# Clearing padding rows on VectorE and ScalarE and reordering the prologue of a fused FFT mixing and SwiGLU kernel

## The chip, the cores and the metric

The kernel runs on one core of one Trainium2 chip. The metric is the device time of one execution in microseconds; a change is judged by the median of several runs. The profile is that of one more execution.

## The reference

```python
def _attn_ref(x):                       # x: 8 x 3008 x 256, float32
    X = np.fft.fft(x, axis=1)
    X = np.fft.fft(X, axis=2)
    return X.real

def _moe_ref(x, w_gate, w_val, w_out):  # x: 24064 x 256; d_ff = 1536
    g = x @ w_gate
    silu = g * (1.0 / (1.0 + np.exp(-g)))
    val = x @ w_val
    return silu * val @ w_out
```

The real part of a two-dimensional Fourier transform of each of the 8 batches is fed, row by row, to a gated feed-forward block. The transform along the 256 columns is linear and can be folded into the two input weight matrices; so the kernel multiplies those once by cosine and sine tables (giving the tiles Wp, Wq and the mirrored Wm) and has only the transform along the 3008 rows left to do per batch.

## The kernel before, in words

**Layout.** The 3008 rows of a batch are folded by symmetry into 188 rows, of which 128 go through the tile XA and 60 through XC. XC holds two batches, 64 partitions each, and 4 partitions of each 64 are padding that has to be zero. Batch 0 has its own small version of XC, called XC0: partitions 0 to 59 and 64 to 123 hold data, 60 and 124 hold the first rows of the sequence, and the remaining padding partitions hold zeros.

**Prologue (about the first 30 us).** All of it is written out by hand, in the order in which each engine executes it.

- SyncE (SP) and ScalarE issue the input transfers. SP: XA upper rows (L247), two of the four XA lower sets (L249), two clears of XC0 padding (L251, copied 64 floats at a time from one row of zeros in the tile `sel`), XC0's pieces (L260), XC0's two first rows (L261), two clears of XC padding (L264), then the loads of batch 1 (L140, L142, L144). ScalarE issues the other two XA sets (L249) and two XC0 pieces (L260). Transfers share eight completion semaphores in rotation, so a queue's later transfer also waits until the earlier one on its semaphore has landed.
- GpSimd makes index rows, the phases `turns` (L332), the products for the small tables (L390 to L394), the placing matrix putC (L395), and issues the first weights (`load_w(0)`, L360); then it folds (`fold_d`, L480) and issues the further weights.
- VectorE makes the phase steps (L301 to L318), the matrix putA (L320), the angles (L336, L340), and later the sums of placed and loaded rows (`sums`, L422: SA for XA, SC for XC0).
- ScalarE makes the sine and cosine tables Tab (L343, L346), their negated part (`opposite`, L352) and weighted part (`weigh_ce`, L355), the small tables CD and SDt (`d_tables`, L402 to L405), the bf16 copies of the folds (EOb, L481) and of XC0's sums (SBc, `halves`, L426 and L427).
- TensorE does warming matmuls (L288, L439), `place` (L413: XA by putA, XC0 by putC), then the first transform, whose even and odd halves (`eo` 0 and 1) each consist of `half_folded` (L468, from EOb) and `unfolded` (L475, from SBc), with `row0` (L581) for one extra row, and `half_w` (L447), which turns the first 512 columns of the two weight matrices into Wp and Wq in two halves. `transform` then copies (L612) and combines (L617) the accumulators into the tiles Pt (even) and Qt (odd).

**Main part.** A planner with costs and due times orders, for 50 tiles of up to 512 columns and 12 blocks of d_ff each, the gate and value products (L904), the activation and products on ScalarE, VectorE and GpSimd, the output products (L1144), the remaining weight transforms (L1335), the folds of later batches and their transforms (L1287). Its first matmul takes Pt and Wp (L904); it follows `half_w(1, 1)` on TensorE. The change doesn't touch it.

The order on TensorE around the change is this, before:

```python
    psC = place(XC0, putC, 2, ((psO, "o"),))
    half_folded(0, 2)
    ...
    for k, (pool, nm) in enumerate(((psV, "v"), (psG, "g"))):
        half_w(0, k, pool, nm)
    ...
    unfolded(0, SBc)
    transform(0, 0, (0,), acc)
    for q in range(2):
        row0(0, q, acc[1][q])
    unfolded(1, SBc)
```

Of the kernel before, what the change touches and what calls it, by code (L numbers as in the profile page):

```python
# [12 lines left out]
F32 = mybir.dt.float32  # L13
I32 = mybir.dt.int32
BF16 = mybir.dt.bfloat16
AF = mybir.ActivationFunctionType
Alu = mybir.AluOpType
# [14 lines left out]
def kernel(  # L32
# [8 lines left out]
    nc = tc.nc  # L41
    B, M, D = x.shape
    Dff = moe_w_gate.shape[1]
    P = 128
# [21 lines left out]
    NCR = GH - P  # L66
# [14 lines left out]
    psG = ctx.enter_context(tc.tile_pool(name="psG", bufs=3, space=bass.MemoryType.PSUM))  # L81
    psV = ctx.enter_context(tc.tile_pool(name="psV", bufs=3, space=bass.MemoryType.PSUM))
    psO = ctx.enter_context(tc.tile_pool(name="psO", bufs=2, space=bass.MemoryType.PSUM))
# [8 lines left out]
    zero = const.tile([P, 1], F32, name="zero")  # L92
    w0 = const.tile([P, 2, nF], F32, name="w0")
    sel = const.tile([P, P], BF16, name="sel")
    CD = const.tile([P, 2, P], BF16, name="CD")
    SDt = const.tile([P, 2, P], BF16, name="SDt")
# [5 lines left out]
    XC = const.tile([P, 8, 2, D], F32, name="XC")  # L102
# [14 lines left out]
    def rows_at(b, row, ap):  # L117
        return bass.AP(tensor=x.tensor, offset=(b * M + row) * D, ap=ap)

    def up_block(b, j, n):  # L120
        return rows_at(b, 2 * j - 1, [[2 * D, n], [R * D, 4], [1, 2 * D]])
# [91 lines left out]
    vts = nc.vector.tensor_scalar  # L213
    vtt = nc.vector.tensor_tensor
    vstt = nc.vector.scalar_tensor_tensor
    pts = nc.gpsimd.tensor_scalar
    ptt = nc.gpsimd.tensor_tensor
# [7 lines left out]
    XC0 = tp.tile([P, 4, 2, D], F32, name="XC0")  # L225
    W0 = [tp.tile([P, 2, T], BF16, name=f"W0{i}") for i in range(2)]
    putA = tp.tile([P, P], F32, name="putA")
    putC = tp.tile([P, P], F32, name="putC")
    df = tp.tile([P, P], F32, name="df")
    prod = tp.tile([P, 2, P], F32, name="prodd")  # L230
    rrd = tp.tile([P, 2, P], F32, name="rrd")
# [3 lines left out]
    q = nc.sync  # L235

    nc.vector.memset(zero, 0.0)
    nc.vector.memset(sel, 0.0)
    nc.scalar.activation(w0[:, 0, 0:1], zero, AF.Silu)
    zrow = sel.bitcast(F32)[1:2, :]  # L240

    def zeros(X, hi):
        dst = X.rearrange("p a q d -> p (a q d)")[64 * hi + NCR:64 * hi + 64, :]
        return dict(out=dst.rearrange("p (k n) -> p k n", n=P // 2),
                    in_=zrow.unsqueeze(1).to_broadcast([1, (64 - NCR) * dst.shape[1] * 2 // P, P // 2]))

    q.dma_start(out=XA3[:, 0:4, :], in_=up_block(0, 1, P))  # L247
    for a, eng in ((3, nc.scalar), (2, q), (1, nc.scalar), (0, q)):
        eng.dma_start(out=XA3[:, 4 + a, :], in_=down_set(0, a, JA, LA, NA))  # L249
    for hi in range(2):  # L250
        q.dma_start(**zeros(XC0, hi))  # L251

    def xc0(hi, what):
        if what == 2:
# [4 lines left out]
    for hi, what in ((0, 2), (1, 2), (0, 0), (1, 0), (0, 1), (1, 1)):  # L259
        (q, nc.scalar)[hi if what != 1 else 0].dma_start(**xc0(hi, what))  # L260
    q.dma_start(out=XC0[NCR:64 + NCR + 1:64, 0:2, 1],  # L261
                in_=rows_at(0, 0, [[2 * R * D, 2], [R * D, 2], [1, D]]))
    for hi in range(2):
        q.dma_start(**zeros(XC, hi))  # L264

    iota = dict(channel_multiplier=0, allow_small_or_imprecise_dtypes=True)
    pcol = tp.tile([P, 1], F32, name="pcol")
    pcol2 = tp.tile([P, 1], F32, name="pcol2")
# [23 lines left out]
    def col(name, n=1, dt=F32):  # L292
        small[name] = tp.tile([P, n], dt, name=name)
        return small[name]
# [12 lines left out]

    m_cols(0, pcol, LA, JA)
    vts(mM[:, 0:2], mm_[:, 0:2], scalar1=1.0 / M, scalar2=None, op0=Alu.mult)
    half = col("half")  # L310
    vts(half, pcol, scalar1=64.0, scalar2=-64.0, op0=Alu.is_ge, op1=Alu.mult)
    pc = col("pc")
# [4 lines left out]
    vtt(mm_[:, 3:4], mm_[:, 3:4], inside, op=Alu.mult)  # L317
    vts(mM[:, 2:4], mm_[:, 2:4], scalar1=1.0 / M, scalar2=None, op0=Alu.mult)  # L318
    nc.vector.memset(halfpi, math.pi / 2.0)
    vts(putA, putA, scalar1=pcol, scalar2=None, op0=Alu.is_equal)  # L320
    nc.vector.memset(EOf[:, 1, :, P:P + 1], 0.0)
    vts(m2, pcol, scalar1=0.0, scalar2=-2.0, op0=Alu.not_equal, op1=Alu.mult)
    vts(sgn, half, scalar1=1.0 / 32, scalar2=1.0, op0=Alu.mult, op1=Alu.add)
# [27 lines left out]
    def opposite(ch):  # L351
        nc.scalar.activation(Tab[:, ch, :, :, NCE:NOO - 1], Tab[:, ch, :, :, GH + 1:NCE], AF.Copy, scale=-1.0)  # L352

    def weigh_ce():
        nc.scalar.activation(Tab[:, 1, 1, :, 0:NCE], Tab[:, 1, 1, :, 0:NCE], AF.Copy, scale=wC)  # L355

    def load_w(fc):
        for i, src in ((0, moe_w_gate), (1, moe_w_val)):
            dst = W0[i] if fc == 0 else Wraw[i][:, :, (fc - 1) * T:fc * T]
            nc.gpsimd.dma_start(out=dst, in_=src.rearrange("(no p) f -> p no f", p=P)[:, :, fc * T:(fc + 1) * T])  # L360
# [15 lines left out]
    def ce_angles(ch):  # L376
        rr, ra = ce_angle[ch]
        angles(rr, kf, ch, ti[ch])
        magnitude(ra, rr)

    def ce_tables(ch):
        rr, ra = ce_angle[ch]
        sine(ch, 0, NCE, rr)
        cosine(ch, 0, NCE, ra)

    ce_angles(0)
    nc.vector.memset(Tab[:, :, :, :, NOO - 1:NOO], 0.0)
    ce_tables(0)
    for i, c_ in enumerate((pcol, pcol2)):
        pts(prod[:, i, :], df, scalar1=c_, scalar2=1.0, op0=Alu.mult, op1=Alu.mult)  # L390
    pts(rad.bitcast(I32), prod, scalar1=1.0 / D, scalar2=1.0, op0=Alu.mult, op1=Alu.mult)
    pts(rrd, rad.bitcast(I32), scalar1=-float(D), scalar2=1.0, op0=Alu.mult, op1=Alu.mult)
    load_w(0)
    ptt(rrd, rrd, prod, op=Alu.add)  # L394
    pts(putC, putC, scalar1=pcol, scalar2=1.0, op0=Alu.is_equal, op1=Alu.mult)  # L395
    ce_angles(1)
    ce_tables(1)
    nc.vector.memset(sel[0:1, :], 1.0)
    scd = 2.0 * math.pi / D * (1.0 - 2e-7)

    def d_tables():
        nc.scalar.activation(rad, rrd, AF.Abs)  # L402
        nc.scalar.activation(CD, rad, AF.Sin, scale=-scd, bias=halfpi)
        nc.scalar.activation(SDt, rrd, AF.Sin, scale=-scd, bias=zero)
        nc.scalar.activation(CD[:, :, 0:1], CD[:, :, 0:1], AF.Copy, scale=0.5)  # L405
# [12 lines left out]
    def sums(S, k, X, pss):  # L418
        n = len(pss)
        for a in range(n):  # L420
            down = X[:, 7 - a] if n == 4 else X[:, 2 + a]
            vtt(S[:, k, a], pss[a], down[:, ::-1, :], op=(Alu.add, Alu.subtract)[k])  # L422

    def halves(SB, S, k, a=0):

        nc.scalar.copy(SB[:, k, 0, a:a + 2], S[:, k, a:a + 2, :, P:0:-1])  # L426
        nc.scalar.activation(SB[:, k, 1, a:a + 2], S[:, k, a:a + 2, :, P:D], AF.Copy, scale=(-1.0 if k else 1.0))  # L427
# [13 lines left out]
    def half_w(h, k, pool, nm):  # L441
        ps = pool.tile([P, 2, T // 2], F32, name=nm)
        dst, tab = ((Wp, CD), (Wq, SDt))[k]
        fs = slice(h * T // 2, (h + 1) * T // 2)
        for gv in range(2):
            for no in range(2):
                nc.tensor.matmul(ps[:, gv, :], tab[:, no, :], W0[gv][:, no, fs], start=(no == 0), stop=(no == 1))  # L447
        if k:
            nc.scalar.copy(dst[:, :, fs], ps)
            pts(Wm[:, :, fs], dst[:, :, fs], scalar1=m2, scalar2=1.0, op0=Alu.mult, op1=Alu.mult)  # L450
        else:
            nc.vector.tensor_copy(dst[:, :, fs], ps)
# [17 lines left out]
    def unfolded(eo, SB):  # L470
        for q in range(2):
            for a in range(2):
                dst, rhs = set_cols(acc[eo][q], Tab[:, 1, q, eo], a)
                for hf in range(2):
                    nc.tensor.matmul(dst, SB[:, eo, hf, a, q, :], rhs, start=False, stop=(a == 1 and hf == 1),  # L475
                                     skip_group_check=True)

    def fold_d(eo, a0):
        s_ = SA[:, eo, a0:a0 + 2]
        ptt(EOA[:, eo, a0:a0 + 2, :, 0:P], s_[:, :, :, P:0:-1], s_[:, :, :, P:D], op=(Alu.add, Alu.subtract)[eo])  # L480
        nc.scalar.copy(EOb[:, eo, a0:a0 + 2], EOA[:, eo, a0:a0 + 2, :, 0:P])  # L481
# [29 lines left out]
    warm(20)  # L511
    sums(SA, 0, XA, psA)
    opposite(0)
    d_tables()
    for a in (0, 2):
        fold_d(0, a)
    sums(SA, 1, XA, psA)
    start_acc(0)
    half_folded(0, 0)
    psC = place(XC0, putC, 2, ((psO, "o"),))  # L520
    half_folded(0, 2)
    weigh_ce()
    opposite(1)
    for a in (0, 2):
        fold_d(1, a)
    load_w(1)
# [2 lines left out]
    start_acc(1)  # L529
    for a in (0, 2):  # L530
        half_folded(1, a)
    nc.vector.memset(SDt[:, :, 0:1], 1.0)
    hd = tp.tile([P, 2, 2, 1], F32, name="hd")
    ptt(hd, SA[:, 0, 0:2, :, 0:1], SA[:, 0, 2:4, :, 0:1], op=Alu.add)
    heads(nc.gpsimd, hd[:, 0], hd[:, 1], CEa)
    nc.gpsimd.tensor_copy(EOA[:, 0, :, :, P:P + 1], SA[:, 0, :, :, 0:1])
    heads(nc.gpsimd, SC[:, 0, 0, :, 0:1], SC[:, 0, 1, :, 0:1], CEc)
    sums(SC, 1, XC0, psC)
    halves(SBc, SC, 1)
    for k, (pool, nm) in enumerate(((psV, "v"), (psG, "g"))):  # L540
        half_w(0, k, pool, nm)
    load_w(2)
    nc.gpsimd.iota(kfO, pattern=[[4, G]], base=1, **iota)
    for ch in range(2):
# [28 lines left out]
    def row0(b, q, ps):  # L573
        CE = coef_a(b)[0]
        todo = [(CE[:, q, 0, k, P:P + 1], Tab[:, 0, q, 0, e], e) for k, e in ((0, E0), (1, E1))]
        if b:
            todo.append((stack_of(b, 0)[:, q, 0, P:P + 1], Tab[:, 1, q, 0, 0:NCE], slice(0, NCE)))
        else:
            todo += [(CEc[:, q, 0, k, 0:1], Tab[:, 1, q, 0, e], e) for k, e in ((0, E0), (1, E1))]
        for l, r_, cols in todo:  # L580
            nc.tensor.matmul(ps[0:1, cols], l, r_, start=False, stop=True, skip_group_check=True)  # L581
# [56 lines left out]
    transform(0, 0, (0,), acc)  # L638
    for q in range(2):
        row0(0, q, acc[1][q])  # L640
    unfolded(1, SBc)
    transform(0, 0, (1,), acc)
    half_w(1, 0, psO, "o")
# [879 lines left out]
```

## Time and profile before

| | |
|---|---|
| Median of 8 runs | 624.19 us (622.86 to 628.66) |
| Profiled execution | 623.59 us |
| Its span, first to last instruction | 621.8 us |
| TensorE busy | 603.8 us (97% of the span) |
| VectorE, ScalarE, GpSimd busy | 577.4, 527.3, 471.3 us |
| Mean granted TensorE clock | 0.994 |

The span is what the trace covers; the execution's own time is 1.8 us longer. A busy share over the whole span says little about the prologue: there TensorE waits for data, and in the rest it is nearly always busy.

### The profile page before, as it was taken

What the parts mean: (1) busy time and instruction counts of PE and PEld (TensorE: products, weight loads), DVE (VectorE), ACT (ScalarE), POOL (GpSimd) and SP (SyncE); (2) the same over time, 40 slices, a digit from 0 to 9 for tenths busy, and PEclk for the clock granted to TensorE, in tenths of its full rate; (3) what the DMA queues carried; (4) which work ended last, traced back from release to release, by engine and by line L of the source; (5) the groups of instructions that cost most, each with busy time, mean ns of one, the idle gap of its engine ahead of it and who ended that gap; (6) DMA issues with size and microseconds to landing.
All of it is one profiled execution on the core that took longest, in us unless ns stands there. A gap on an engine that the chain in (4) does not pass through costs nothing.

```text
span 621.8 us, 12518 instructions
## 1 busy us (share of the span) xinstructions
PE 603.8 (97%) x4012; PEld 395.4 (64%) x4073; DVE 577.4 (93%) x1054; ACT 527.3 (85%) x1001; POOL 471.3 (76%) x432
## 2 busy tenths in 40 slices
PE   7899989999999999999999999999999999999997
PEld 4445656666666666666666666666666666666676
DVE  7499969999999999999999999999999999999982
ACT  5487556789889899898898899998998988999994
POOL 8599688899797888987888778877787444446652
PEclk9799999999999999999999999999999999999999
DMA  9762545544523613454144122125121111211112
GB/s 222 103 109 57 157 113 153 151 137 118 146 61 89 142 45 105 131 136 130 50 102 137 52 58 76 57 68 164 45 60 52 45 50 46 61 41 56 59 52 78
DMA packets 51340, 57.74 MB, mean 93 GB/s; under 512 B 8002, under 2 KB 38346, under 8 KB 51274
## 3 DMA queue, kind: packets, MB, share of 16 engines
q1 hardware_dynamic: 47592, 53.69, 32.0%
q0 software_dynamic: 3184, 2.36, 3.0%
q10 hardware_dynamic: 498, 0.89, 0.5%
q8 instruction: 32, 0.52, 0.4%
q14 instruction: 34, 0.28, 0.2%
HBM read 29.39 MB, written 24.65 MB: 87 GB/s over the span
## 4 chain that ended last, share of the span: by engine, by line
PE 84%; DVE 6%; DMA 3%; issue 2%; SPq 2%; POOL 2%; ACT 2%; DVEq 0%; ACTq 0%; POOLq 0%
PE o L1144 35%; PE g L904 22%; PE v L904 19%; DVE es L1027 2%; PE g L1287 2%; PE o L1287 2%; DMA XC<-in_x_dram 1%; DMA XA<-in_x_dram 1%; DVE sv L1088 1%; SPq L142 1%; PE v L1144 1%; PE o L413 1%; SPq L140 1%; PE g L581 1%; DVE hp L942 0%
## 5 line engine op out<-in xcount | busy, mean ns | idle before, releaser
L1095 POOL TENSOR_TENSOR hm<-sv 128x1024 bf16<-128x1024 f32 (+2 forms) x133 | 247.3, 1860 | 120.0 <-ACT sv L1074 67.6
L1088 DVE SCALAR_TENSOR_TENSOR sv<-es,v 128x512 f32<-128x512 f32 (+2 forms) x266 | 178.0, 670 | 1.7 <-issue 0.6
L1098 DVE TENSOR_TENSOR hp<-sp,v 128x512 bf16<-128x512 f32 (+2 forms) x260 | 174.2, 670 | 3.2 <-ACT sp L1071 2.4
L1144 PE MATMUL o<-Wo,hm 128*128 128x256 bf16 (+1 forms) x1128 | 166.4, 273 | 0.7
L1144 PE MATMUL o<-Wo,hp 128*128 128x256 bf16 (+1 forms) x1104 | 165.6, 273 | 0.4
L1144 PEld LDWEIGHTS <-hp 128*128 128x128 bf16 (+2 forms) x1140 | 112.1, 99 | 62.5 <-issue 4.2
L1144 PEld LDWEIGHTS <-hm 128*128 128x128 bf16 (+2 forms) x1140 | 112.0, 98 | 61.3 <-issue 0.4
L1002 ACT ACTIVATE sp<-g 128x512 f32<-128x512 f32 (+2 forms) x202 | 119.8, 594 | 32.9 <-PE g L904 21.6
L1074 ACT ACTIVATE sv<-g 128x512 f32<-128x512 f32 (+2 forms) x202 | 131.5, 652 | 7.7 <-PE g L904 5.1
L904 PE MATMUL v<-Pt,Wp 128*128 128x512 bf16 (+2 forms) x283 | 106.0, 375 | 2.4 <-DVE hp L1098 0.9
L1027 DVE SCALAR_TENSOR_TENSOR es<-bc,w,v 128x512 f32<-128x512 bf16 (+2 forms) x140 | 102.0, 731 | 5.2 <-DMA bc<-br 3.6
L904 PE MATMUL g<-Pt,Wp 128*128 128x512 bf16 (+2 forms) x284 | 106.4, 375 | 0.3
L904 PE MATMUL g<-Qt,Wq 128*128 128x512 bf16 (+2 forms) x242 | 90.5, 374 | 0.3
L976 ACT ACTIVATE v<-bc,w 128x512 f32<-128x512 bf16 (+2 forms) x126 | 87.2, 692 | 0.4 <-DVE hp L1098 0.3
L904 PE MATMUL g<-Qt,Wm 128*128 128x512 bf16 (+2 forms) x219 | 82.0, 374 | 0.2
L1025 ACT COPY es<-v 128x512 f32<-128x512 f32 (+2 forms) x126 | 73.5, 583 | 3.2 <-PE v L904 2.7
L904 PEld LDWEIGHTS <-Wp 128*128 128x128 bf16 x576 | 56.2, 98 | 30.6 <-issue 4.8
L904 PE MATMUL v<-Qt,Wq 128*128 128x512 bf16 (+2 forms) x162 | 60.7, 375 | 2.3 <-DVE es L1027 2.1
L904 PEld LDWEIGHTS <-Wq 128*128 128x128 bf16 x450 | 44.0, 98 | 21.5 <-issue 1.3
L1150 ACT COPY ev<-o 128x512 f32<-128x512 f32 x89 | 53.3, 599 | 4.1 <-PE o L1144 2.7
L904 PE MATMUL v<-Qt,Wm 128*128 128x512 bf16 (+2 forms) x148 | 55.4, 374 | 0.5 <-DVE hp L942 0.5
L904 PEld LDWEIGHTS <-Wm 128*128 128x128 bf16 x372 | 36.4, 98 | 17.8 <-issue 0.2
(191 smaller groups left out, 706.4 us busy)
## 6 DMA issues: line engine op xcount, KB each, us to landing
out_dram<-ev SPq DMA_DIRECT2D x96, 128.0 KB
XA<-in_x_dram SPq DMA_DIRECT2D x30, 256.0 KB
XA<-in_x_dram SPq DMA_DIRECT2D x112, 64.0 KB
XC<-in_x_dram SPq DMA_DIRECT2D x31, 120.0 KB
XC<-in_x_dram SPq DMA_DIRECT2D x105, 32.0 KB
bc<-br SPq DMA_DIRECT2D x21, 128.0 KB
St<-Fc SPq DMA_DIRECT2D x14, 128.5 KB
out_dram<-ev SPq DMA_DIRECT2D x12, 120.0 KB
```

Source lines behind the costliest of these rows:

```text
L904: nc.tensor.matmul(ps[:, :n], Wt[:, gv, fs], src[:, :n], start=start, stop=stop, skip_group_check=True)
L976: nc.scalar.activation(T_[kv][:, :w], bc[t][:, :w], AF.Copy, scale=w0[:, 1, f:f + 1])
L1002: nc.scalar.activation(T_[ksp][:, :w], T_[kg][:, :w], AF.Silu)
L1025: nc.scalar.copy(T_[kes][:, :w], T_[kv][:, :w])
L1027: nc.vector.scalar_tensor_tensor(T_[kes][:, :w], bc[t][:, :w], w0[:, 1, f:f + 1], T_[kv][:, :w], op0=Alu.mult, op1=Alu.add)
L1074: nc.scalar.activation(sv()[:, f % 2, w - 1::-1, 1], T_[kgm if by_dve else kg][:, :w], AF.Silu)
L1088: nc.vector.scalar_tensor_tensor(sv()[:, f % 2, w - 1::-1, 0], T_[kes][:, :w], 2.0, T_[kv][:, :w], op0=Alu.mult, op1=Alu.subtract)
L1095: nc.gpsimd.tensor_tensor(hts_(t)[1][:, f - 1:f + 1, :w], sv()[:, :, :w, 1], sv()[:, :, :w, 0], op=Alu.mult)
L1098: nc.vector.tensor_tensor(hts_(t)[0][:, f, :wp], T_[ksp][:, :wp], T_[kv][:, :wp], op=Alu.mult)
L1144: nc.tensor.matmul(st["ps"][:n, j, :], hts[t][minus][:, f, c:c + n], Wo[:, f, :], start=(f == 0), stop=(f == nF - 1))
L1150: nc.scalar.copy(ev[:, 0:len(pair), :], st["ps"][:, 0:len(pair), :])
L1287: nc.tensor.matmul(st[q][:, cols], l, r_, start=(i == 0), stop=(i == len(mms) - 1), skip_group_check=True)
```

## The change

1. The padding rows of XC0 are no longer cleared by two transfers. VectorE clears the first half of the whole tile's columns, ScalarE copies a zero column over the second half, and the transfers of XC0's data are issued after that. The rows of XC are cleared by four transfers with runs of 2048 floats, copied from XC0's row 61, instead of two with runs of 64 floats from `sel`.
2. The products of the small tables move from GpSimd to ScalarE, the compare that makes putC from GpSimd to VectorE, the compare that makes putA further ahead on VectorE, and the first weights' issue behind the last step of the small tables' phases on GpSimd.
3. On ScalarE, `weigh_ce` and `opposite(1)` come ahead of the folds' copies, and `d_tables` comes after the first two of them. The clearing of SDt's first column moves behind the last sums on VectorE.
4. On TensorE, `half_w(0, 0)` and `half_w(0, 1)` move from ahead of the even half's `unfolded` to behind `row0`, between the two halves of the first transform; their results go to the PSUM pool psO instead of psV and psG.

```diff
     nc.vector.memset(zero, 0.0)
     nc.vector.memset(sel, 0.0)
+    xf = XC0.rearrange("p a q d -> p (a q d)")
+    nc.vector.memset(xf[:, 0:4 * D], 0.0)
     nc.scalar.activation(w0[:, 0, 0:1], zero, AF.Silu)
-    zrow = sel.bitcast(F32)[1:2, :]
-
-    def zeros(X, hi):
-        dst = X.rearrange("p a q d -> p (a q d)")[64 * hi + NCR:64 * hi + 64, :]
-        return dict(out=dst.rearrange("p (k n) -> p k n", n=P // 2),
-                    in_=zrow.unsqueeze(1).to_broadcast([1, (64 - NCR) * dst.shape[1] * 2 // P, P // 2]))
-
     q.dma_start(out=XA3[:, 0:4, :], in_=up_block(0, 1, P))
     for a, eng in ((3, nc.scalar), (2, q), (1, nc.scalar), (0, q)):
         eng.dma_start(out=XA3[:, 4 + a, :], in_=down_set(0, a, JA, LA, NA))
-    for hi in range(2):
-        q.dma_start(**zeros(XC0, hi))
+    nc.scalar.copy(xf[:, 4 * D:8 * D], zero.to_broadcast([P, 4 * D]))
...
     q.dma_start(out=XC0[NCR:64 + NCR + 1:64, 0:2, 1],
                 in_=rows_at(0, 0, [[2 * R * D, 2], [R * D, 2], [1, D]]))
+    X3c = XC.rearrange("p a q d -> p (a q d)")
     for hi in range(2):
-        q.dma_start(**zeros(XC, hi))
+        for k in range(2):
+            q.dma_start(out=X3c[64 * hi + NCR:64 * hi + 64, 8 * D * k:8 * D * (k + 1)],
+                        in_=xf[NCR + 1:NCR + 2, :].unsqueeze(1).to_broadcast([1, 64 - NCR, 8 * D]))
...
     vts(mM[:, 0:2], mm_[:, 0:2], scalar1=1.0 / M, scalar2=None, op0=Alu.mult)
+    vts(putA, putA, scalar1=pcol, scalar2=None, op0=Alu.is_equal)
...
-    vts(putA, putA, scalar1=pcol, scalar2=None, op0=Alu.is_equal)
...
+    for i, c_ in enumerate((pcol, pcol2)):
+        nc.scalar.activation(prod[:, i, :], df, AF.Copy, scale=c_)
     ce_angles(0)
     nc.vector.memset(Tab[:, :, :, :, NOO - 1:NOO], 0.0)
     ce_tables(0)
-    for i, c_ in enumerate((pcol, pcol2)):
-        pts(prod[:, i, :], df, scalar1=c_, scalar2=1.0, op0=Alu.mult, op1=Alu.mult)
     pts(rad.bitcast(I32), prod, scalar1=1.0 / D, scalar2=1.0, op0=Alu.mult, op1=Alu.mult)
     pts(rrd, rad.bitcast(I32), scalar1=-float(D), scalar2=1.0, op0=Alu.mult, op1=Alu.mult)
+    ptt(rrd, rrd, prod, op=Alu.add)
     load_w(0)
-    ptt(rrd, rrd, prod, op=Alu.add)
-    pts(putC, putC, scalar1=pcol, scalar2=1.0, op0=Alu.is_equal, op1=Alu.mult)
     ce_angles(1)
+    vts(putC, putC, scalar1=pcol, scalar2=None, op0=Alu.is_equal)
     ce_tables(1)
...
     opposite(0)
-    d_tables()
+    weigh_ce()
+    opposite(1)
     for a in (0, 2):
         fold_d(0, a)
+    d_tables()
     sums(SA, 1, XA, psA)
...
     half_folded(0, 2)
-    weigh_ce()
-    opposite(1)
...
-    nc.vector.memset(SDt[:, :, 0:1], 1.0)
...
     sums(SC, 1, XC0, psC)
+    nc.vector.memset(SDt[:, :, 0:1], 1.0)
     halves(SBc, SC, 1)
-    for k, (pool, nm) in enumerate(((psV, "v"), (psG, "g"))):
-        half_w(0, k, pool, nm)
     load_w(2)
...
     for q in range(2):
         row0(0, q, acc[1][q])
+    for k in range(2):
+        half_w(0, k, psO, "o")
     unfolded(1, SBc)
     transform(0, 0, (1,), acc)
     half_w(1, 0, psO, "o")
```

## The prediction

> **What bounds the kernel now.** The page first.
>
> ```profile
> span 621.8 us, 12518 instructions
> PE 603.8 (97%) x4012; PEld 395.4 (64%) x4073; DVE 577.4 (93%) x1054; ACT 527.3 (85%) x1001; POOL 471.3 (76%) x432
> ```
>
> TensorE lacks 18 us of work in the whole span. The table of stretches shows where (after the stretch and its length: PE, weight loads, VectorE, ScalarE, GpSimd busy, clock, DMA share, GB/s):
>
> ```profile
> 6.90:13.90 7.00, 6.96 (x32) 3.52 (x32) 5.13 (x10) 4.74 (x9) 6.39 (x9) 1.00 1.17 219
> 13.90:18.10 4.20, 0.03 (x1) 0.02 (x1) 1.23 (x3) 3.30 (x5) 3.89 (x7) 0.82 0.76 162
> 18.10:23.40 5.30, 5.29 (x10) 2.22 (x11) 2.19 (x5) 0.77 (x2) 0.79 (x5) 0.50 1.07 94
> 23.40:29.60 6.20, 6.20 (x48) 4.18 (x46) 2.83 (x10) 3.07 (x6) 3.27 (x6) 1.00 0.41 86
> 29.60:45.00 15.40, 14.30 (x87) 6.48 (x87) 15.22 (x28) 12.94 (x25) 14.98 (x27) 1.00 0.75 127
> ```
>
> Two things are to be seen: 4.2 us without TensorE work, then 5.3 us at half its clock. What ended the wait, by the timeline of TensorE and the waits of SyncE's queue:
>
> ```profile
> 18.11 3.75 PE L413 MATMUL o<-XC,putC 128*128 128x512 f32 x4 [4.19 <-POOL hd L534]
> ...
> 21.66 0.84 PE L468 MATMUL v<-Tab,EOb 128*128 128x377 bf16 x2
> ```
> ```profile
> SPq L251 <- DMA XA<-in_x_dram: 3.3, 1, 3.3
> SPq L260 <- DMA XA<-in_x_dram: 1.8, 2, 1.4
> SPq L261 <- DMA XC<-sel: 1.3, 1, 1.3
> ```
>
> The releaser named, hd, is not read by that matmul; of GpSimd it needs putC, done at 11.35. It also waits for XC0's last transfer, L261, whose semaphore ends at 17.84 in the trace. L261 was issued at 13.95, after waiting for the cleared rows (XC<-sel). So placing XC0 is the late step, and SyncE's queue made it late:
>
> ```profile
> 2.71 4.79 SPq L251 DMA_DIRECT2D XC<-sel  x2
> 7.93 4.57 SPq L260 DMA_DIRECT2D XC<-in_x_dram  x4
> 13.95 0.61 SPq L261 DMA_DIRECT2D XC<-in_x_dram  x1
> 14.60 1.43 SPq L264 DMA_DIRECT2D XC<-sel  x2
> ```
>
> From 18.11 to 28.94 the chain that ended last is TensorE without a break; then VectorE's Qt, and at 30.06 the first L904 matmul that needs Qt. After 45 us TensorE is busy 14.95 of 15.00 us. A shorter prologue therefore reaches the end, if VectorE and GpSimd, full from 29.6 to 45, move with it.
>
> **What the skill says.** "TensorE: Matmul & The Clock Gate", Part 1: the clock halves after about one idle window of 3.4 us and returns after a busy one. The trace agrees: 4.19 us idle, and the clock is 0.50 until about 23.4. "DMA: Bandwidth & Descriptors", Queues, rings and completion order: all queues share the same 16 engines, which serve them in turn by packets. Here all three queues carried data between 8 and 18 us. The same page, Why small descriptors are slow: a fixed cost per piece. Agrees: the 768 pieces of 256 bytes took 46 ns each, the 2048-byte ones 113 ns, 8 times the bytes in 2.5 times the time.
>
> **The change, part by part.**
>
> *SyncE.* L251 goes (two issues of 0.75 and the 3.3 us wait). The first XC0 piece is issued at 2.7 instead of 7.93. The next three now wait, through shared semaphores, for XA's upper rows, L249's sets 3 and 1 (landed 6.80, 7.92, 9.74): issued at 6.9, 8.0, 9.8, the last instead of 11.66. L261 follows at 10.7 instead of 13.95, since no cleared row is waited for. Behind it four clears at about 0.7 each, each waiting for a landing of 11 to 13 us, then batch 1's loads at about 14.5 instead of 16.07. XA itself is ahead in the same queues: unchanged.
>
> *When XC0 is complete.* XA and XC0 are 3.0 MB; from 2.5 us at the 290 GB/s of those slices they would be in at 12.8, plus 0.5 to the semaphore: 13.3, the early end. The first weights (1 MB read) start near 11 and share the engines; if they all go first, at 300 GB/s, 16.6. That is also near before's order: there, pieces issued from 9.75 landed only behind the weights. Both ends are estimates from the trace; I take the middle, **14.9 against 17.84**.
>
> *VectorE.* Clearing 1024 floats: "VectorE: DVE Perf Modes", Zero memsets, gives one cycle (0.96 GHz) per element: 1.07 us, an estimate; the nearest row, 64 elements in 0.11 us, would extrapolate to 1.76; 0.5 if it ran twice as fast. I take 1.07. It delays the phase steps, so `turns` by 0.9 (GpSimd was busy to 2.07 anyway), the angles and ScalarE's first table from 5.39 to 6.4. putC's compare adds 0.28 (putA's row) before the sums: the first ends at 10.1 instead of 9.7, the second still starts at 10.34 on TensorE's data. So sums unchanged.
>
> *ScalarE.* The copy of 1024 zeros: "ScalarE: Activation LUTs", What ACT_TABLE_LOAD costs, 186 ns + 0.833 per element: 1.04, an estimate (its 512 gives 0.61, the trace 0.62). It ends at 3.3, where the second piece's issue started before (3.23). Two products, 0.3 each, end at 4.9, before the tables' inputs. Four tables, both opposites and weigh_ce (0.93, 0.91, 0.93, 0.91, 0.82, 0.92, 0.84, overlapping by 0.1) run 6.4 to 12.6; the first EOb copy starts at 12.6 instead of 12.43. d_tables (1.5) fits between second and third copy, 14.5 to 16.0; copies three and four end at 17.1 instead of 17.28. Cost: 0.2 at 12.6, hidden behind TensorE's wait for XC0; if XC0 came at 13.3 this chain would be the limit (below).
>
> *GpSimd.* Loses the products (1.25) and putC (0.75), gains 0.9 of lateness: the first weights are issued at 9.0 instead of 8.21, the first fold starts at 11.1 instead of 11.31. Folds depend on VectorE's sums: unchanged. The later Wm products lie behind `turns`: 20.4 to 23.2, Wm at 23.2 and 24.4, Wo's issue at 25.1 instead of 32.11.
>
> *TensorE.* Place: at full clock a matmul is 0.86 (L413 rows at 10.13 and 10.99), so 1.9 for two instead of 3.75. Twelve L468: 0.32 a pair, 1.9 instead of 2.75. With the gap 14.9 - 13.9 = 1 us no idle window arises. `half_w` (0.88) comes out ahead of unfolded(0) and goes in ahead of unfolded(1): zero for Qt.
>
> **Sum.** 14.9 + 1.9 + 1.9 = 18.7 for the end of the half_folded matmuls, against 24.62. ScalarE: second XC0 sum at 17.5, two SBc copies (1.15) to 18.7: the same moment. With 0.1 for the semaphore, 18.8: 24.62 - 18.8 = **5.8 us**. By parts: 2.9 arrival and 3.0 clock. The limit of ScalarE's chain, 17.1 + 1.15, makes 6.3 the most. From there the order is as before; the first Qt matmul comes at 24.3 instead of 30.06. GpSimd moves by 7.0, VectorE by 5.8. The main part's instructions are the same; new waits there are for the four clears, landed long before. I take off 0.2 for joints: 5.6. The profiled execution would go from 623.59 to 618.0; the median of the runs is 0.6 above it: 624.19 - 5.6 = **618.6**.
>
> **Rivals.**
>
> *Weights ahead of XC0* (0.20). For: before, the XC0 pieces landed behind the weights on every engine. Against: they are issued 2 us earlier now, and the weights 0.8 later. At 16.6 the gain is 5.8 - 1.7 = 4.1, 620.1; if the 2.7 us gap halves the clock for one window, 1.7 less: 2.4, 621.8.
>
> *Something else sets the start* (0.06). GpSimd has no idle between 26.9 and 64.5; if its list did not move, TensorE would meet it at the first L1287 (47.7) and the gain would be 0, 624.2. Against: each of its steps waits only for things that move.
>
> *The first weights become the bound; slower* (0.07). `half_w` now stands ahead of unfolded(1) in TensorE's queue, at 20.9 where it was at 24.46, and the weights start later. From a landing after 20.9 all behind it waits; after 26.7 the kernel is slower. Before, they landed at 15.58 and 17.25; the slowest weight transfer of the prologue took 10.6 us, which from 9.9 gives 20.5, just inside. Sharing with XC0's and batch 1's pieces would have to double it: landing at 29 gives 626.5.
>
> **How the numbers follow.** The forecast, with XC0 in at 13.3 to 15.6 (5.1 to 6.3, plus half a microsecond of scatter: 617.2 to 619.5), has 0.67. The range 617.0 to 622.0 takes in the first rival and leaves out about 0.15. 0.3% (1.9 us) is about what a measurement of this kernel can tell from no change; faster by more: 0.67 + 0.20 = 0.87; within: 0.06; slower: 0.07.
>
> **What would show it.** Right: place on XC0 starts near 14.9; clock 1.00 from 13 to 25; L468 to L475 without a gap; `half_w` not waiting; first Qt matmul near 24.3; stretches after that as before, 5 to 6 us earlier. Wrong: place after 16.6 (first rival); 0.50 in the clock column; an idle PE before L444 (`half_w`'s line there) waiting for W (third); or an early first Qt matmul with the difference lost before 60 us (second).

## The result and the profile after

| | before | after |
|---|---|---|
| Median of the runs compared | 625.22 us | 621.63 us (616.83 to 623.26) |
| Ratio, 95% interval | | 0.9932 (0.9913 to 0.9951) |
| Profiled execution, its span | 623.59, 621.8 us | 621.69, 619.8 us |
| XC0's last transfer landed | 17.84 us | 16.21 us |
| Placing of XC0 starts | 18.11 us | 16.41 us |
| Clock halved in the prologue | 16.60 to 23.43 | 17.05 to 20.47 |
| First product of the main part, first with Qt | 29.63, 30.06 us | 27.00, 27.24 us |
| TensorE's wait near 84 us | 1.83 us | 3.47 us |

The kernel is faster by 0.68%, 4.2 us of 625.2, with an interval of 3.1 to 5.4; the forecast was 5.6. Before ran at 625.2 here where the runs shown ahead had 624.19, so the ratio is the measure. The same two lines of the page, then the same stretches:

```profile
span 619.8 us, 12523 instructions
PE 603.0 (97%) x4012; PEld 395.0 (64%) x4073; DVE 578.0 (93%) x1056; ACT 528.8 (85%) x1004; POOL 469.4 (76%) x429
```

```profile
6.90:13.90 7.00, 6.55 (x30) 3.20 (x30) 6.83 (x13) 6.28 (x8) 5.94 (x9) 1.00 1.09 266
13.90:18.10 4.20, 2.23 (x7) 0.93 (x6) 1.46 (x4) 2.97 (x7) 3.89 (x7) 0.88 0.54 84
18.10:23.40 5.30, 5.30 (x25) 2.40 (x24) 2.44 (x6) 2.78 (x5) 3.38 (x10) 0.78 0.95 151
23.40:29.60 6.20, 6.15 (x44) 4.00 (x43) 5.10 (x16) 3.31 (x6) 3.90 (x6) 1.00 0.70 140
```

The stretch that had 0.03 us of TensorE work has 2.23, and the one at clock 0.50 has 0.78: a shorter wait and one halved window instead of two. Neither is gone. TensorE's timeline around the wait, and SyncE's queue:

```profile
13.96 0.48 PE L465 MATMUL g<-Tab,EOb 128*128 128x377 bf16 x2
16.41 3.13 PE L410 MATMUL o<-XC,putC 128*128 128x512 f32 x4 [1.97 <-POOL EOA L477]
19.33 0.84 PE L465 MATMUL v<-Tab,EOb 128*128 128x377 bf16 x2
...
21.50 0.48 PE L465 MATMUL g<-Tab,EOb 128*128 128x377 bf16 x2
21.82 0.80 PE L472 MATMUL v<-Tab,SBc 128*128 128x377 bf16 x4
...
23.96 0.61 PE L444 MATMUL o<-W,CD 128*128 128x256 bf16 x4
```

```profile
2.73 7.64 SPq L254 DMA_DIRECT2D XC<-in_x_dram  x4
10.41 0.59 SPq L255 DMA_DIRECT2D XC<-in_x_dram  x1
11.04 2.78 SPq L260 DMA_DIRECT2D XC<-XC  x4
13.87 6.07 SPq L140 DMA_DIRECT2D XC<-in_x_dram  x8
```

What that queue waited for up to 30 us (total, times, longest):

```profile
SPq L254 <- DMA XA<-in_x_dram: 4.1, 2, 3.1
SPq L140 <- DMA XC<-in_x_dram: 3.6, 6, 1.5
SPq L140 <- DMA XC<-XC: 1.9, 4, 0.9
```

The wait for cleared rows ahead of the last piece is gone; XC0's pieces now wait for XA's sets, and the clears of XC are waited for behind them, by batch 1's loads.

The releaser named at 16.41, EOA, is as little read by that matmul as hd was before. In the five executions with the new clears in which TensorE waited for XC0 (this one, a3, c1, b2 and d1 below) it starts 0.20 or 0.21 us after the landing of L255, which was L261 before. SyncE did what was forecast: L255 went out at 10.41 (forecast 10.7, before 13.95). Its data took until 16.21, and TensorE then placed at half speed for most of the time. Later the gain shrinks once more, at the tile bc: it holds the first row of tile 2 spread over all partitions, comes by two transfers (br<-Qt, then bc<-br), and VectorE's product es reads it. VectorE's timeline at its first use, and TensorE's behind it:

```profile
82.83 1.41 DVE L1024 SCALAR_TENSOR_TENSOR es<-bc,w,v 128x512 f32<-128x512 bf16 x2 [5.22 <-DMA bc<-br]
```

```profile
79.78 0.38 PE L901 MATMUL g<-Qt,Wm 128*128 128x512 bf16 x1
83.63 0.38 PE L901 MATMUL v<-Qt,Wq 128*128 128x512 bf16 x1 [3.47 <-DVE es L1024]
```

From 27 to 56 us the matmuls are 2.7 us earlier than before, just ahead of this wait 3.3, behind it 1.6, at the end 2.0. The transfer comes from SyncE, whose queue issues 52 transfers from 53 to 83 us: 22 us of issuing, with waits between. At 53 us this queue was 2.7 us earlier than before, from 69 us on 2.0, and so was the issue of bc (79.98 against 82.00). In between lies an output store whose issue took 1.63 us, against 0.54 before; what held it the trace doesn't name.

### The profile page after: what moved, and what is told of

It is laid out like the page before. It is cut to its first block, busy times and chain, and to the rows that moved or that the text cites. A ratio compares the mean times of both kernels' runs of the same rounds, so it can differ in the third digit from the quotient of the medians.

```text
span 619.8 us, 12523 instructions
## 1 busy us (share of the span) xinstructions
PE 603.0 (97%) x4012; PEld 395.0 (64%) x4073; DVE 578.0 (93%) x1056; ACT 528.8 (85%) x1004; POOL 469.4 (76%) x429
## 4 chain that ended last, share of the span: by engine, by line
PE 87%; DVE 6%; DMA 2%; issue 2%; SPq 1%; ACT 1%; POOL 0%; DVEq 0%; ACTq 0%
PE o L1141 37%; PE g L901 23%; PE v L901 19%; DVE es L1024 2%; PE g L1284 2%; PE o L1284 2%; DMA XA<-in_x_dram 1%; DVE sv L1085 1%; PE v L1141 1%; DVE hp L939 1%; PE g L576 1%; PE o L410 1%; PE o L576 0%; DVE XA L333 0%; SPq L142 0%
```

## The experiments

Theory: the gain is XC0's earlier arrival; the missing 1.4 us is the halved clock and the late half of the arrival (the first weights share the DMA engines), and part of it leaks at the wait for bc. Rivals: other chains hide the prologue's TensorE time; the moves, not the clears, bring the gain; XC0's own pieces set its arrival. What each profiled execution showed (us):

| run | ratio to before (95%) | XC0 in | placing | clock halved up to 100 us | wait at bc | first product |
|---|---|---|---|---|---|---|
| a1_warm | 0.9947 (0.9916 to 0.9977) | 15.54 | 15.86 | 80.3 to 83.7 | 2.56 | 24.79 |
| b1_warm | 0.9983 (0.9967 to 1.0000) | 19.29 | 19.53 | 14.0 to 17.4, 85.7 to 89.1 | 3.92 | 28.43 |
| a2_w0late | 1.0002 (0.9977 to 1.0028) | 13.39 | 14.30 | 23.8 to 30.6, 88.6 to 95.5 | 5.34 | 31.45 |
| a3_halfw_back | 0.9960 (0.9942 to 0.9978) | 15.64 | 15.84 | 15.3 to 18.7, 83.6 to 90.4 | 4.32 | 26.17 |
| c1_after_bc | 0.9922 (0.9895 to 0.9949) | 16.17 | 16.37 | 16.1 to 19.5 | none | 26.88 |
| c2_before_bc | 0.9980 (0.9964 to 0.9995) | 19.08 | 19.32 | 15.3 to 25.5 | none | 31.27 |
| b2_clears_only | 0.9948 (0.9923 to 0.9974) | 15.67 | 15.88 | 14.6 to 18.1, 82.9 to 86.3 | 3.72 | 25.85 |
| a6_bc_w0mid | 0.9914 (0.9881 to 0.9946) | 13.36 | 14.29 | none | none | 25.77 |
| d1_bc_warm | 0.9886 (0.9854 to 0.9918) | 16.16 | 16.36 | none | none | 25.31 |
| a4_old_clears | 1.0001 (0.9978 to 1.0024) | 19.26 | 19.50 | 17.2 to 24.1 | 2.21 | 30.65 |
| d2_best | 0.9885 (0.9853 to 0.9918) | 13.56 | 14.30 | none | none | 24.98 |

**a1_warm: fill the wait.**

```diff
     half_folded(0, 0)
+    warm(28)
     psC = place(XC0, putC, 2, ((psO, "o"),))
```

> The changed kernel with 28 more warming matmuls (about 1.8 us of TensorE work) between the half_folded matmuls of the first fold and the placing of XC0, so that TensorE is not idle while it waits for XC0's last transfer. In the profiled run of the changed kernel that wait is 1.97 us, and the clock is 0.50 for the 3.4 us after it. Theory A (the missing part of the forecast is the halved clock after this wait): the clock stays 1.00 to 25 us, the half_folded matmuls end 1.5 to 1.9 us earlier, near 20.2, and the time is about 619.5 to 620.0 where the changed kernel's profiled run had 621.7; the runs scatter less. Theory B (only the late arrival of XC0 matters, TensorE's speed behind it is hidden by other chains): within 0.4 us of the changed kernel.

In the profiled execution the prologue did what theory A says: clock full, placing in 1.94 us, first product 2.2 us earlier than in the changed kernel. TensorE's timeline:

```profile
14.30 1.72 PE L436 MATMUL o<-sel 128*128 128x128 bf16 x28
15.86 1.94 PE L410 MATMUL o<-XC,putC 128*128 128x512 f32 x4
17.63 0.48 PE L465 MATMUL v<-Tab,EOb 128*128 128x377 bf16 x2
```

But the timed runs gained nothing over the changed kernel, and they scattered over 7 us, not less. The profile says where it can go: up to 77 us the matmuls stand 4.9 to 5.5 us ahead of before; then TensorE waits 2.56 us for bc and runs a window at half clock, and 3.2 are left. In this execution theory A is half right: the clock's gain is there, and another wait takes it. That the same happened in the timed runs is not shown here.

**b1_warm: the same in before.**

```diff
     half_folded(0, 0)
+    warm(60)
     psC = place(XC0, putC, 2, ((psO, "o"),))
```

> The kernel before with 60 more warming matmuls (about 3.8 us) at the same place, ahead of the placing of XC0; nothing else is changed. It takes the clock alone and leaves the arrival of XC0 at 17.84. The clock's part in the forecast was 3.0 us. Theory A (the halved clock behind the 4.19 us wait is worth what the durations say): placing takes 1.9 instead of 3.75 and the twelve half_folded matmuls 1.9 instead of 2.75 us, so 2.4 to 3.0 us less than the kernel before, about 621.5. Theory B (ScalarE's copies and the folds end at about the same moment anyway, so that a faster TensorE there only waits): less than 0.8 us gained.

A gain of 0.17%, 1.1 us, between the two. It doesn't decide: TensorE had already waited 2.73 us before 13.58, so most of the filling itself ran at half clock (4.94 us for 60 matmuls, where 28 at full clock took 1.72), and it lasted until XC0's late landing at 19.29. Placing and half_folded behind it ran at full clock. What the clock alone is worth in before stays open.

**a2_w0late: first weights behind everything.**

```diff
-    load_w(0)
     ce_angles(1)
...
+    load_w(0)
     load_w(1)
     sums(SC, 0, XC0, psC)
```

> The changed kernel with the issue of the first weights moved on GpSimd from ahead of ce_angles(1) to just ahead of the issue of the next weights, behind the folds, so that no weights are read while XC0 comes in. Theory A (XC0 comes late, at 16.2 instead of the 13.3 of the early end, because the first weights share the DMA engines): XC0's last transfer lands at 13.3 to 14.5, TensorE's wait there shrinks from 1.97 us to under 0.6, no halved clock follows, and the time falls by 2 to 3 us to about 619. Theory B (XC0's time is set by its own pieces and by the shared semaphores of SyncE's queue): it lands within 0.4 of 16.2 and the time stays. Against both: the first weights may come after 24 us, where half_w needs them; then TensorE waits ahead of half_w and the gain is lost or turned round.

XC0 lands at 13.39, though its last transfer was issued no earlier (10.57 against 10.41), and TensorE doesn't wait for it: sharing with the first weights is what makes it late, and theory B is out. The packets agree: from 12 to 13 us the weights' queue has 179 in the changed kernel and SyncE's 19; here SyncE's has 64, and the weights' none. The price is the other one named. TensorE's timeline:

```profile
20.55 0.33 PE L576 MATMUL g<-Tab,CEc 128*1 128x189 bf16 x2
23.55 0.40 PE L443 MATMUL o<-W,CD 128*128 128x256 bf16 x2 [2.67 <-DMA W<-in_moe_w_gate_dram]
```

A second wait of 2.83 follows for the other half, at half clock, and the whole gain is gone: the mechanism of the prediction's slower rival, had here by an edit.

**a3_halfw_back: half_w in its old place.**

```diff
+    for k, (pool, nm) in enumerate(((psV, "v"), (psG, "g"))):
+        half_w(0, k, pool, nm)
     load_w(2)
...
-    for k in range(2):
-        half_w(0, k, psO, "o")
     unfolded(1, SBc)
```

> The changed kernel with half_w(0, 0) and half_w(0, 1) put back ahead of the even half's unfolded, in the PSUM pools psV and psG; the rest of the change stays. The prediction costed this move at zero for Qt, because the same matmuls only change sides of unfolded(0). Theory A (zero): within 0.3 us of the changed kernel, first Qt matmul at 27.2. Theory B (the move covers TensorE's wait for the copies of XC0's sums or for the weights): with it undone the even half starts 0.9 us later and VectorE makes Pt later, but the even half now waits less for SBc; between 0.5 us better and 1.0 us worse.

0.28% above the changed kernel, 1.75 us, with overlapping intervals. That is more than either theory expected, and no loss of this size is shown or excluded. The profiled execution has no such loss in the prologue: its first product came at 26.17 instead of 27.00, 0.83 earlier, and its half_folded matmuls had ended 0.83 earlier already (21.16 against 21.99).

**c1_after_bc and c2_before_bc: tile 2's row earlier, in both kernels.**

```diff
-            if k >= 0 and fr == {0: 11, 2: 99}.get(tr, 6) and tr + 1 < nT:
+            if k >= 0 and fr == {0: 11, 1: 2, 2: 99}.get(tr, 6) and tr + 1 < nT:
```

> The changed kernel with one number of the planner changed: the two transfers that spread the first row of tile 2 over all partitions (br<-Qt, then bc<-br) are given to SyncE's queue four blocks of d_ff earlier (at the third block of tile 1 instead of the seventh). In the profiled run of the changed kernel TensorE waits 3.47 us near 83.6 us for VectorE's es, which waits for bc. Theory A (the gain of the prologue is partly given back at this wait, and by the halved clock that follows it in some runs): the wait is gone, bc lands some 10 us before it is needed, and the time is 2 to 4.5 us below the changed kernel's, at 617 to 619.5. Theory B (SyncE's queue is full from about 53 to 83 us, so that whatever is behind the two moved transfers is late instead): another wait of 2 us or more between 60 and 110 us, time within 1 us of the changed kernel's.

> The kernel before with the same number of the planner changed as in the run above. TensorE waits 1.83 us at this place in the profiled run of before, and more in others. Theory A (what was gained in the prologue leaks out at this wait): with it gone in both kernels the difference of the two is what the prologue gained, 3 us and, with the clock full in both or halved in both, up to 5; this kernel alone is 1.5 to 3 us below the kernel before. Theory B: within 1 us of the kernel before, and the difference of the pair stays at about 3.5 us.

bc is issued at 60.77 instead of 79.98, and VectorE's first es on tile 2 no longer waits (its timeline):

```profile
77.41 1.40 DVE L1024 SCALAR_TENSOR_TENSOR es<-bc,w,v 128x512 f32<-128x512 bf16 x2
```

No wait of a microsecond is left behind the prologue in either, so SyncE's queue did not make another late. In the profiled execution of c1 the gain grows to 4.4 us at this place and stays there. But the medians say less than theory A: c2 gains 0.2% on before, 1.2 us, and c1 0.1% on the changed kernel, not distinguishable. The quotient of the two, 0.9922 / 0.9980, is 0.9942, 3.6 us, about the change's 4.2. So the wait for bc costs the kernel before, and perhaps the changed one; that it takes this change's gain in particular is not shown.

**b2_clears_only and a4_old_clears: the change in two halves.** b2 is before with item 1 of the change alone, of which this is the part for XC0:

```diff
+    nc.vector.memset(xf[:, 0:4 * D], 0.0)
...
-    for hi in range(2):
-        q.dma_start(**zeros(XC0, hi))
+    nc.scalar.copy(xf[:, 4 * D:8 * D], zero.to_broadcast([P, 4 * D]))
```

> The kernel before with the new clears alone: VectorE and ScalarE clear XC0, its transfers are issued behind that, the rows of XC are cleared by four transfers with long runs; nothing is moved on GpSimd, ScalarE or TensorE. Theory A (the gain is the earlier issue of XC0 and the arrival that follows, as the prediction has it): XC0's last transfer lands at 15.5 to 16.5 instead of 17.84, the wait for it shrinks by 1.5 to 2.5 us, and most of the gain is here: 2 to 4 us below the kernel before. Theory B (the reordering on GpSimd, ScalarE and TensorE is what matters): less than 1 us below it. The products that stay on GpSimd keep its first weights at their old place, 0.8 us earlier than in the changed kernel, so these compete with XC0 a little more.

> The changed kernel with the clears of before: two transfers for XC0 and two for XC, from sel; everything that the change moved on GpSimd, ScalarE and TensorE stays moved. The clears alone gave 0.9948 of before, the whole change 0.9932. Theory A (the clears are the gain, the moves are worth the 0.1 to 0.2% between): XC0 in at 17.3 to 18.2 as before, and 0.997 to 1.0 of before. Theory B (the two halves overlap, either alone brings most of it): 0.994 to 0.996.

b2 lands XC0 at 15.67 and gains 0.52%; a4, all moves without the clears, gains nothing (1.0001): its XC0 is in at 19.26, a microsecond later than expected, and TensorE waits 5.84 us for it. TensorE's timelines, b2 first:

```profile
14.40 0.61 PE L465 MATMUL v<-Tab,EOb 128*128 128x377 bf16 x2 [3.26 <-ACT EOb L478]
14.80 0.84 PE L465 MATMUL g<-Tab,EOb 128*128 128x377 bf16 x2
15.88 3.03 PE L410 MATMUL o<-XC,putC 128*128 128x512 f32 x4 [0.23 <-POOL EOA L477]
```

```profile
19.50 3.75 PE L413 MATMUL o<-XC,putC 128*128 128x512 f32 x4 [5.84 <-DMA XC<-in_x_dram]
```

In b2 the wait itself lies elsewhere: TensorE waits 3.26 us for ScalarE's first EOb copy, and hardly for XC0 after that. In the timed runs theory A holds in both: the gain is the clears. What the moves add is within the intervals. Not separated is the second part of item 1, the four clears of XC with long runs in place of two with short ones; they are issued behind XC0's last transfer in both kernels.

**a6_bc_w0mid: first weights near 14 us.**

```diff
-    load_w(0)
     ce_angles(1)
...
     for a in (0, 2):
         fold_d(0, a)
+    load_w(0)
     d_tables()
```

(beside c1's edit)

> The changed kernel with the two transfers of tile 2's first row given earlier as in the first run of this set, and with the first weights issued on GpSimd behind the first two folds, near 14 us, instead of at 9.2. With the first weights behind everything XC0 was in at 13.4 instead of 15.5 to 16.2, but the weights then came at 23.5 and 26.8 where half_w needed them near 21. Theory A (there is room between): XC0 in at 13.4 to 14, no wait for it and no halved clock there, weights in at 19.5 to 22; the first Qt matmul near 24, and 1 to 3 us below the first run of this set. Theory B (batch 1's loads, issued from 14 us on, hold up weights issued behind them): weights after 23, TensorE waits ahead of half_w, and the time is that of the first run or 1 to 3 us above it. The two late issues of 0.8 us also delay the third fold by 1.7.

XC0 in at 13.36, no wait for it, no halved clock; the second half of the weights landed at 22.91, and TensorE waited once:

```profile
21.06 0.39 PE L443 MATMUL o<-W,CD 128*128 128x256 bf16 x2
22.95 0.38 PE L443 MATMUL o<-W,CD 128*128 128x256 bf16 x2 [1.50 <-DMA W<-in_moe_w_val_dram]
```

First product at 25.77, 1.1 us ahead of c1. The ratio is 0.08% below c1's: theory A in the profile, no difference that the timed runs can tell.

**d1_bc_warm: a1's and c1's edits together.**

> The changed kernel with both: the transfers of tile 2's first row four blocks earlier, and the 28 warming matmuls ahead of the placing of XC0. With the warming alone the first Qt matmul came at 25.0 in the profiled run, 2.2 us earlier, but TensorE then waited 2.56 us at bc and ran a window at half clock, and the timed runs showed no gain over the changed kernel. Theory A (the prologue's clock is worth 1.5 to 2 us, and it was the wait at bc, later by as much, that took it back): with that wait gone the gain stays, 1.3 to 2.3 us below the changed kernel with the early transfers alone (0.9922 of before), so 0.988 to 0.990. Theory B (the warming shifts the halved clock to other places, or its benefit is chance of one run): within 0.7 us of 0.9922.

0.9886, inside what theory A expected. No halved clock up to the last microseconds, no wait over 0.9 us behind the prologue, and the 6.0 us that the matmuls are ahead of before at 140 us are there at the end. It looks as if filling the wait for XC0 pays once the wait for bc can't take it back; but the intervals of d1 and c1 overlap, so the 2.3 us between them are likely rather than shown.

**d2_best: a6 with half_w behind the odd half.**

```diff
-    for k in range(2):
-        half_w(0, k, psO, "o")
     unfolded(1, SBc)
     transform(0, 0, (1,), acc)
+    for k, (pool, nm) in enumerate(((psV, "v"), (psG, "g"))):
+        half_w(0, k, pool, nm)
```

> The kernel with early transfers of tile 2's first row and the first weights issued near 14 us, and with half_w(0, 0) and half_w(0, 1) moved behind the odd half's unfolded (pools psV and psG). In the run without this move TensorE waited 1.5 us for the first weights ahead of half_w; behind unfolded(1) they are needed 1.45 us later. Theory A (that wait is on the path): it shrinks to under 0.3 us, the first matmul of the main part comes at 24.9 to 25.2 instead of 25.77, and the time is 0.5 to 0.9 us lower. Theory B (VectorE's and ScalarE's copies of the four half_w results then come in one lump behind Qt, and the first matmul that reads Wq waits for them): first matmul at 25.7 or later, no gain.

The wait for the weights is gone, and half of theory B's came in its place (TensorE's timeline):

```profile
22.36 0.60 PE L443 MATMUL v<-W,CD 128*128 128x256 bf16 x4
...
24.98 0.38 PE L901 MATMUL g<-Pt,Wp 128*128 128x480 bf16 x1 [0.70 <-DVE Wp L448]
```

The first product is 0.8 earlier. At 0.9885, 7.2 us below before, this and d1 are the fastest, 0.5% below the changed kernel, with intervals that just overlap the changed kernel's. Its prologue has no stretch at half clock:

```profile
13.90:18.10 4.20, 3.81 (x17) 1.61 (x16) 3.45 (x7) 2.99 (x8) 4.17 (x6) 1.00 0.72 95
18.10:23.40 5.30, 5.22 (x38) 3.24 (x39) 1.63 (x10) 2.80 (x6) 5.08 (x13) 1.00 1.01 167
```

## Why the prediction was right, and where it was off

The side and the first half of the mechanism were right: the clears leave SyncE's queue, XC0's last transfer is issued 3.5 us earlier, and this brings the gain (b2, a4). But its landing came 1.6 us earlier instead of 2.9, and the clock was not kept. The measured 621.6 lies in the range of 617.0 to 622.0 and outside the forecast's own 617.2 to 619.5: it lies where the first rival stood, for whose sake the range was that wide. The size was 5.6 for 4.2 us, and that it came so near was in part luck (see the base). By its steps:

- **SyncE** was right to 0.4 us: pieces at 2.73, 6.54, 7.65 and 9.53, L255 at 10.41; batch 1's loads came at 13.87, 0.6 ahead of the forecast.
- **The small costs** were right or too high, and hidden behind the wait for XC0. VectorE's clear took 0.91 us, less than the 1.07 worked out from one cycle per element; here the measurement decides. ScalarE's copy took 1.04 (1.04). The EOb copies began at 12.98 (12.6) and ended at 17.0 (17.1). half_w did not wait; what its move is worth a3 leaves open. The moves are worth nothing without the clears (a4).
- **When XC0 is complete: 14.9 was the middle of two ends, and execution sits at an end.** With the first weights issued at 9.2 to 9.5 it was in at 15.5 to 16.2 in six kernels; with them issued behind it, at 13.4 to 13.6 in three. The early end (13.3) was well worked out, the late one (16.6) somewhat too late; averaging them was the error, and the first rival described what happened. The rule on shared engines that the prediction took from the Trainium skill ("DMA: Bandwidth & Descriptors", Queues, rings and completion order) fits what a2 and a6 show: the weights, whose issue began 1.2 us before L255's, kept it back by 2 to 3 us.
- **Clock: "no idle window arises" was wrong.** It rested on a gap of 1.0 us, and the gap was 1.97. It also read the trace of before too kindly, as a whole idle window: there the clock fell at 16.60, 2.7 us into the wait. In the changed kernel the clock was halved from 17.05 to 20.47. From the start of placing to the end of the half_folded matmuls it took 16.41 to 21.99, 5.6 us instead of 3.8. Together: the forecast's 18.8 against 21.99 is 3.2 late, 1.5 from the start of placing and 1.8 from the clock, less 0.1 for the semaphore that the sum had added. The first rival's own price for this, 1.7, was the right one. (Of the 3.0 us that the sum put down to the clock, 0.27 was the time from landing to placing in before; the durations alone give 2.7.)
- **Joints: 0.2 was too little** for the profiled pair. Of 2.8 us at the first Qt matmul 2.0 were left at the end; the difference went at the wait for bc, which stood in the trace of before with 1.83 us and was read over. The second rival, a loss before 60 us, did not happen: the lead was 2.7 us from 27 to 56 us.
- **The base, and luck.** By profiled executions alone the change brought 1.9 us, by the timed runs 4.2. The profiled execution of before was a good one: XC0 landed at 17.84, while in the three kernels with the old clears above it landed at 19.1 to 19.3. From 19.2 to 15.9, the middles of these groups, the arrival is worth 3.3 us; this is a likely share of the 4.2, not a measured one. So a forecast that came 3.2 us late in the changed kernel was partly made good by a kernel before that is mostly slower than the execution it was reckoned from.

How often clock is lost can be read from the mean granted clock of each timed run. A half-clock stretch of 3.41 us takes 0.0028 off the mean of a span of 620 us. Of the changed kernel's twelve runs two had 0.999 and 1.000 and took 616.8 and 617.7 us; three had 0.997 and took 620.2 to 621.7; seven had 0.991 to 0.995, about two or three lost stretches, and took 621.2 to 623.3. So the runs that lost none are below the forecast's 618.6, and most runs lose two or more. The runs don't say where, nor how much is the clock and how much the waits that go with it. Of the 47 runs of before that stand against a1, the middle one had 0.991, about three stretches.

The pair d1 and c2, with the clock kept full by the filling in d1 and bc out of the way in both, fits the forecast's size as what the prologue holds: 0.9886 / 0.9980 is 0.9906, 5.9 us, but its interval is wide (some 3.6 to 8) and takes in the change's 4.2. Open stays what the halved clock alone costs before (b1).

## What to carry to other kernels

Where two transfers share the DMA engines, forecast the arrival as one of two times by which is issued first, and order the issues by need. A wait ahead of TensorE has two prices, its length and possibly 1.7 us (an estimate: half of 3.41) for a window at half clock behind it; removing the wait, or filling it with throwaway matmuls, kept the clock full in the profiles of a6, d1 and d2 up to the last microseconds, with the early bc. Before a gain at the start is booked, follow it to each later place where TensorE waits for an in-order queue: it can be given back there, as in the profiles of the changed kernel and a1.

## What the runs showed of the hardware that was not expected

The clock falls with less than a whole idle window. In the thirteen profiled executions (before, after and the eleven above) the half-clock stretches lie on a fixed grid of 3.41 us that has another phase in each execution. From 10 us on, each window at full clock in which TensorE was idle for 1.97 us or more was followed by a half-clock window (14 cases ahead of the kernels' last microseconds, among them 1.97 in after, 2.34 in a1, 2.68 in before, 3.21 in b1 and the whole 3.41 in a4), and none with 1.80 us or less was. Several waits in one window add up: in a3 1.73 us of waiting for ScalarE's first copy and 0.87 for XC0 made 2.60, and the clock fell. And the same wait can cost a window or not: the changed kernel's 3.47 us near 82 us lay across a boundary, in windows that were idle for 1.80 and 1.72 us, and the clock stayed at 1.00; a1's 2.56 us put 2.34 into one window and halved the next. "TensorE: Matmul & The Clock Gate", Part 1, says that the window is free-running, which the phases agree with; its "idle window" is, by these traces, a window idle for somewhat over half.
